# Weight loads moved from SyncE's queue to GpSimd's, and the order of the last four VectorE steps, in a fused attention and gated-FFN kernel

## The chip, the core and the metric

The kernel runs on one core of a Trainium2 chip. A core has TensorE (matrix products), VectorE, ScalarE and GpSimd (elementwise work and reductions) and SyncE, which here only issues DMAs. Each engine has a queue of its own, worked off in order; they meet at semaphores. SyncE, ScalarE and GpSimd can issue DMAs, and all DMAs of the core run on the same 16 DMA engines. The metric is the device time of one execution in microseconds (us).

## The reference

The output is `x + s * silu(r)`, with `x` of 2048 tokens by 640, `xn = layernorm(x)`, `s` an attention and `r` a small routed feed-forward block. All arrays are bf16.

```python
xn = _layernorm(x)
# A: attention against the last W = 512 rows of a cache, 32 heads of 192
q = (xn @ wq).reshape(B, Sq, 32, 192).transpose(0, 2, 1, 3)
scores = einsum("bhqd,bhkd->bhqk", q, k_cache[:, :, -512:]) * 192 ** -0.5
o = einsum("bhqk,bhkd->bhqd", softmax(scores), v_cache[:, :, -512:])
s = o.transpose(0, 2, 1, 3).reshape(B, Sq, 6144) @ wo
# B: the two tokens with the largest r go through a gated FFN of width 1536
r = xn @ w_r
idx = argsort(-r)[:, :2]
y = (silu(xn[idx] @ w_gate) * (xn[idx] @ w_up)) @ w_down
g = silu(xn + scatter_add(zeros, idx, y * sigmoid(r[idx])))
return x + s * g
```

## The kernel before

**The main loop.** The 32 heads are worked in 8 groups of 4. A group has 4 blocks of 512 tokens by 2 pairs of heads; each of these 64 steps is cut in two *halves* of 256 tokens, 128 halves in all, numbered k. A group is 16 halves. In half k TensorE makes the scores (`quad`, L296 to L303), VectorE the row maxima (L314), ScalarE the exponentials (L321, tile `pexp`). SyncE then issues one DMA transpose of `pexp` into `pT` (L327). Two halves later TensorE multiplies `pT` with the values (`o_products`, L339), VectorE scales the result (L353, `o_sb`), and SyncE issues its transpose `oT` (L357). Six halves later the output projection runs (`w_item`, L386 and L388) and VectorE adds it to `s_acc` (L394). The queries of the next step (L263, L268) are made in between. `pexp` has two buffers, so the exponentials of half k + 2 wait until the transpose of half k has landed.

**The order of the work** is written out by hand: `FIRST` and `LAST` list the steps of the ends as tokens, and in the loop between, each half runs what was put into the lists `mid[k]` and `bg[k]`. An engine's queue follows the order of the program. Nothing reorders it.

**SyncE's queue** carries nearly all DMAs: the transposes `pT`, `oT` and `kT` (the last turns the raw keys of the next group, L125), and the next group's loads, spread over the halves of the group: `wq_g` (L110), `k_raw` (L104), `v_sb` (L115), `wo_g` (L120). `kT`, `v_sb` and most of `wo_g` share the same few halves of each group.

**The routed block** is spread over halves 11 to 103. Its buffers are in two pools of one buffer each per tag; in the pool `moe_w` the candidates, the weights of each FFN block (`wgu`), those of the down projection (`wd`) and the broadcast result (`y_bc`) all have the tag `w`, that is, one buffer used in turn. GpSimd issues the gather of the two tokens (`xg`, L616, in half 33). Then, for each of three blocks `fb` of 512 columns, ten loads of 128 KB (`m_ffn_piece`, L626) fill `wgu`, one or two in a half, from halves 37, 44 and 52; the products with `wgu` (`m_ffn`, L666) run in halves 43, 51 and 58. Twelve loads of 160 KB (`m_wd_piece`, L684) fill `wd` in halves 59 to 66, and `m_down` uses it in half 68. `m_sum` then sends the result to all partitions by two DMAs of GpSimd (`y_d` L713, `y_bc` L715). From half 71 GpSimd adds it to `xn` (L719 to L723), from half 109 it multiplies and adds for the output (L782, L783).

**The end.** The last tokens' output rows are made by `last`: a `W` token is the projection (TensorE, L856), `m` the product with the gate `xn` (VectorE, L862, which reads the projection's PSUM), `a` the sum with `s_acc` on VectorE and `g` the same sum on GpSimd (both L866), each followed by SyncE's store (L867). The last 128 tokens are cut into two column halves, `127.0` and `127.1`, of 320 each.

The lists that place the loads:

```python
    pieces = {0: (2, 2, 2, 2, 2), 1: (1, 1, 2, 2, 2, 2), 2: (2, 2, 2, 2, 2)}
    for fb, (k0, km) in enumerate(((37, 43), (44, 51), (52, 58))):
        q = 0
        for h, n in enumerate(pieces[fb]):
            for _ in range(n):
                bg[k0 + h].append(m_ffn_piece(fb, q))
                q += 1
        mul, turn = m_ffn(fb)
        bg[km].append(mul)
        bg[km + 1].append(turn)
    q = 0
    for h, n in enumerate((1, 1, 1, 2, 2, 2, 2, 1)):
        for _ in range(n):
            bg[59 + h].append(m_wd_piece(q))
            q += 1
```

Of the kernel before, what the change touches and what calls it, by code (L numbers as in the profile page):

```python
# [21 lines left out]
def kernel(ctx, tc, A_x, A_k_cache, A_v_cache, A_wq, A_wo, B_x, B_w_r, B_w_gate, B_w_up, B_w_down, out):  # L22
    nc = tc.nc
    P = 128
# [4 lines left out]
    W = min(4096, max(256, Sk // 4))  # L29
# [113 lines left out]
    for _ in range(22):  # L143
# [5 lines left out]
        out=ident_f, in_=ident_f, compare_op=ALU.not_equal, fill=1.0, base=0,  # L149
# [373 lines left out]
    M = {}  # L523
# [96 lines left out]
    def m_ffn_piece(fb, q):  # L620
        def f():
            if q == 0:
                M["wgu"] = M["w"].tile([P, 2, DC, 512], BF16, name="wgu", tag="w")
            w, dc = divmod(q, DC)
            src = (B_w_gate, B_w_up)[w].rearrange("(c p) f -> p c f", p=P)
            nc.sync.dma_start(out=M["wgu"][:, w, dc, :], in_=src[:, dc, fb * 512:(fb + 1) * 512])  # L626
        return f

    def m_gather():
# [50 lines left out]
    def m_wd_piece(q):  # L680
        def f():
            if q == 0:
                M["wd"] = M["w"].tile([P, FC, D], BF16, name="wd", tag="w")
            nc.sync.dma_start(out=M["wd"][:, q, :], in_=B_w_down.rearrange("(c p) d -> p c d", p=P)[:, q, :])  # L684
        return f

    def m_sig():
# [58 lines left out]
    for fb, (k0, km) in enumerate(((37, 43), (44, 51), (52, 58))):  # L746
        q = 0
# [7 lines left out]
    q = 0  # L755
# [114 lines left out]
    S M.0 M.1 E.0 M.2 O.125.0 o.125.0 M.3 E.1 W.121.w m.121 a.121 R.127 O.125.1 o.125.1 C  # L870
    O.126.0 W.122.t O.126.1 o.126.0 m.122 o.126.1 g.122 W.123.w T.126 m.123
    O.127.0 o.127.0 O.127.1 o.127.1 g.123 W.124.t m.124 T.127 g.124 W.125.w m.125 g.125
    W.126.t m.126 g.126 W.127.0.h W.127.1.h m.127.0 a.127.0 m.127.1 a.127.1
    """.split()
    for token in LAST:
        last(token)
# [31 lines left out]
```

## Time and profile before

| | |
|---|---|
| median of 3 runs | 820.8 us (818.43 to 821.37) |
| the profiled execution | 818.35 us, its span 816.6 us |
| TensorE | 800.6 us busy, 98% |
| VectorE, ScalarE | 629.2 us (77%), 485.5 us (59%) |
| GpSimd | 203.1 us (25%) |
| DMA queue q1 (SyncE's) | 138.26 MB, 90.1% of the 16 engines' span |
| DMA queue q0 (GpSimd's) | 2.01 MB, 1.0% |
| SyncE's issues of wgu, wd | 30 of 128 KB, 12 of 160 KB; median 0.43 us each, landing 2.9 to 3.1 us after |
| SyncE's issue of pT | 126, 1.3 to 4.0 us, median 2.7; landing 4.2 to 7.6 us after, median 4.8 |

How to read the lines of the profile: times are us from the start of the span unless marked ns. PE is TensorE, PEld its weight loads, DVE VectorE, ACT ScalarE, POOL GpSimd, SP SyncE; a q behind a name is the engine's sequencer, which waits and issues. `L327` is a line of the kernel. `pT<-pexp` is what an instruction writes and reads. In a timeline a line has the start, the duration, the engine, line, operation, tiles and count, and in brackets the idle time of the engine before it and what ended that. In a line of stretches come the stretch, its length, then for PE, PEld, DVE, ACT and POOL the busy time and in brackets the number of instructions, then TensorE's granted clock, the DMA engines' busy share and GB/s. In the slices each digit is a fortieth of the span, in tenths (9 is 90% or more). A DMA queue has its packets, MB and share of the 16 engines' span.

### The profile page before, as it was taken

To read this page: it belongs to the slowest core of one execution; us is meant where nothing else is said; L and a number is where in the kernel's file an instruction comes from. 1 tells how busy PE (TensorE), PEld (TensorE's weight loads), DVE (VectorE), ACT (ScalarE), POOL (GpSimd) and SP (SyncE) were. 2 spreads that over 40 slices of the span, in tenths; PEclk is the share of its full clock that TensorE was granted. 3 is DMA by queue.
4 is the path that set the end of the run, shared out by engine and by line. 5 is a ranking of instruction groups with operands and counts; after the bars stand their busy time and mean duration, and the time that the engine had idled before them with its cause. 6 is when DMAs were issued, how large, how long until landed. Compare 5 with 4: busy or idle time off the path is not lost. (4 is left out here: it accounts for less than half of the span.)

```text
span 816.6 us, 15427 instructions
## 1 busy us (share of the span) xinstructions
PE 800.6 (98%) x5786; PEld 446.3 (55%) x5786; DVE 629.2 (77%) x1250; ACT 485.5 (59%) x1271; POOL 203.1 (25%) x151
## 2 busy tenths in 40 slices
PE   8889999999999999999999999999999999999997
PEld 4455555555555555555555555555555555555555
DVE  7988688887877776777676777777988877767886
ACT  5677565565565555556655665665676765655652
POOL 0001000000000000000000799999900001452533
PEclk9999999999999999999999999999999999999999
DMA  8889999989989999999999889887998879977984
GB/s 239 163 160 182 185 174 187 179 162 180 170 155 169 186 194 186 181 192 193 203 183 183 167 170 192 157 146 140 190 180 149 159 144 194 200 155 156 178 161 115
DMA packets 440427, 142.07 MB, mean 174 GB/s; under 512 B 413452, under 2 KB 439952, under 8 KB 440352
## 3 DMA queue, kind: packets, MB, share of 16 engines
q1 hardware_dynamic: 438720, 138.26, 90.1%
q0 software_dynamic: 688, 2.01, 1.0%
q8 instruction: 45, 0.74, 0.4%
q10 hardware_dynamic: 944, 0.82, 0.3%
q14 instruction: 30, 0.25, 0.1%
HBM read 39.98 MB, written 2.62 MB: 52 GB/s over the span
## 5 line engine op out<-in xcount | busy, mean ns | idle before, releaser
L321 ACT ACTIVATE pexp<-s,nm 128x512 bf16<-128x512 f32 x512 | 348.3, 691 | 257.3 <-DVE nm L314 162.2
L314 DVE TENSOR_REDUCE nm<-s 128x1 f32<-128x512 f32 x512 | 319.0, 683 | 56.0 <-PE s L303 55.9
L263 PE MATMUL q_ps<-xnT,wq_g 128*128 128x512 bf16 x945 | 234.7, 380 | 0.9 <-DMA xnT<-xn 0.7
L339 PE MATMUL o_ps<-v_sb,pT 128*128 128x192 bf16 x2048 | 210.3, 246 | 2.9 <-DMA pT<-pexp 1.3
L339 PEld LDWEIGHTS <-pT 128*128 128x128 bf16 x2048 | 173.1, 98 | 50.1 <-issue 6.1
L386 PE MATMUL w_ps<-wo_g,oT 128*128 128x512 bf16 x726 | 176.4, 379 | 0.0
L353 DVE TENSOR_TENSOR o_sb<-o_ps,lsum 128x384 bf16<-128x384 f32 x248 | 135.2, 545 | 47.0 <-PE o_ps L339 46.9
L263 PEld LDWEIGHTS <-wq_g 128*128 128x128 bf16 x945 | 80.3, 98 | 119.9 <-issue 50.1
L268 ACT ACTIVATE qT<-q_ps 128x512 bf16<-128x512 f32 x185 | 110.0, 596 | 40.1 <-PE q_ps L263 39.9
L394 DVE TENSOR_TENSOR s_acc<-s_acc,w_ps 128x640 f32<-128x640 f32 x96 | 78.8, 821 | 59.1 <-PE w_ps L388 58.8
L321 ACT ACTIVATION_READ_ACCUMULATOR pexp<-s,nm 128x1 f32 x512 | 106.2, 207 | 0.0
L386 PEld LDWEIGHTS <-oT 128*128 128x128 bf16 x726 | 69.1, 98 | 57.1
L297 PE MATMUL s<-kT,qT 128*128 128x512 bf16 x256 | 97.0, 379 | 1.9 <-ACT pexp L321 1.2
L296 PE MATMUL s<-kT,qT 128*128 128x512 bf16 x256 | 97.1, 379 | 0.6 <-ACT pexp L321 0.6
L302 PE MATMUL s<-kT,qT 64*128 64x512 bf16 x256 | 77.1, 381 | 0.0
L303 PE MATMUL s<-kT,qT 64*128 64x512 bf16 x256 | 77.1, 381 | 0.0
L388 PEld LDWEIGHTS <-oT 128*128 128x128 bf16 x726 | 50.7, 98 | 28.6
L722 POOL TENSOR_SCALAR yh<-y_bc,oh 128x640 bf16<-128x640 bf16 x32 | 61.3, 1916 | 3.3 <-DMA y_bc<-y_d 1.7
L388 PE MATMUL w_ps<-wo_g,oT 128*128 128x128 bf16 x726 | 60.3, 219 | 0.0
L713 POOL DMA_DIRECT2D y_d<-y_sb x1 | 0.6, 581 | 226.7 <-DVE y_sb L711 226.7
L723 POOL TENSOR_TENSOR xn<-xn,yh 128x640 bf16<-128x640 bf16 x32 | 44.6, 1394 | 2.7
L302 PEld LDWEIGHTS <-qT 64*128 64x128 bf16 x256 | 14.1, 94 | 56.3 <-issue 56.3
(134 smaller groups left out, 388.6 us busy)
## 6 DMA issues: line engine op xcount, KB each, us to landing
wo_g<-in_A_wo_dram SPq DMA_DIRECT2D x48, 160.0 KB, 2.9
wq_g<-in_A_wq_dram SPq DMA_DIRECT2D x35, 192.0 KB, 3.0
k_raw<-in_A_k_cache_dram SPq DMA_DIRECT2D x32, 192.0 KB, 3.0
v_sb<-in_A_v_cache_dram SPq DMA_DIRECT2D x32, 192.0 KB, 2.9
x_fin<-in_A_x_dram SPq DMA_DIRECT2D x16, 160.0 KB, 3.0
pT<-pexp SPq DMA_TRANSPOSE x130, 4.8
oT<-o_sb SPq DMA_TRANSPOSE x126, 3.2
wgu<-in_B_w_gate_dram SPq DMA_DIRECT2D x15, 128.0 KB, 3.0
```

The source lines that it names most:

```text
L263: nc.tensor.matmul(q_ps, lhsT=grp[g]["wq"][:, dc, col0:col0 + P], rhs=xnT[:, t5 * 4:(t5 + 1) * 4, dc, :], start=(dc == 0), stop=(dc == DC ...
L268: nc.scalar.activation(out=qT_of[i][:, c, :], in_=q_ps, func=ACT.Copy, scale=scale)
L296: nc.tensor.matmul(s0, lhsT=qT[:, 0, ssl], rhs=kp[:, :, 0, :], start=True, stop=False)
L297: nc.tensor.matmul(s1, lhsT=qT[:, 2, ssl], rhs=kp[:, :, 2, :], start=True, stop=False)
L302: nc.tensor.matmul(s0, lhsT=qT[0:64, 1, ssl], rhs=kp[0:64, :, 1, :], start=False, stop=True)
L314: nc.vector.tensor_reduce(out=nm_of[k][:, c:c + 1], in_=tiles[c // 2][c % 2], axis=AX.X, op=ALU.max, negate=True)
L321: nc.scalar.activation(out=pexp[:, u, hh, :], in_=tiles[u][hh], func=ACT.Exp, bias=nm[:, c:c + 1], scale=1.0, accum_out=l_of[k][:, c:c + 1])
L339: nc.tensor.matmul(o_ps[:, hh, :], lhsT=pT_of[k][:, u, hh, j, :], rhs=grp[g]["v"][:, 2 * pr + hh, j, :], start=(j == 0), stop=(j == NJ - 1))
L353: nc.vector.tensor_tensor(out=o_sb[:, u], in0=o_ps, in1=l_of[k][:, 2 * u:2 * u + 2].unsqueeze(2).to_broadcast([P, 2, Dh]), op=ALU.mult)
L386: nc.tensor.matmul(w_ps[:, 0:DA], lhsT=oT[:, c // 3, u % 2, c % 3, :], rhs=wo_g[:, c, 0:DA], start=(c == 0), stop=(c == CPG - 1))
L388: nc.tensor.matmul(w_ps[:, DA:D], lhsT=oT[:, c // 3, u % 2, c % 3, :], rhs=wo_g[:, c, DA:D], start=(c == 0), stop=(c == CPG - 1))
L394: nc.vector.tensor_tensor(out=s_acc[:, n, :], in0=s_acc[:, n, :], in1=w_ps, op=ALU.add)
```

## The change

The ten loads of each `wgu` set and the twelve of `wd` are issued by GpSimd instead of SyncE; their place in the program is the same. In `LAST` the product of the second column half comes before the sum of the first.

```diff
@@ m_ffn_piece
-            nc.sync.dma_start(out=M["wgu"][:, w, dc, :], in_=src[:, dc, fb * 512:(fb + 1) * 512])
+            nc.gpsimd.dma_start(out=M["wgu"][:, w, dc, :], in_=src[:, dc, fb * 512:(fb + 1) * 512])
@@ m_wd_piece
-            nc.sync.dma_start(out=M["wd"][:, q, :], in_=B_w_down.rearrange("(c p) d -> p c d", p=P)[:, q, :])
+            nc.gpsimd.dma_start(out=M["wd"][:, q, :], in_=B_w_down.rearrange("(c p) d -> p c d", p=P)[:, q, :])
@@ LAST
-    W.126.t m.126 g.126 W.127.0.h W.127.1.h m.127.0 a.127.0 m.127.1 a.127.1
+    W.126.t m.126 g.126 W.127.0.h W.127.1.h m.127.0 m.127.1 a.127.0 a.127.1
```

## The prediction

> **What bounds the kernel now.** I read four views, in this order: the page's slices, the busy time by stretch, the waits of the stretch in which the moved loads run, and the order of time around the one stall found there. First the slices, as tenths of the span: TensorE busy, its granted clock, then the DMA engines, and below them what the queues moved.
>
> ```profile
> PE   8889999999999999999999999999999999999997
> PEclk9999999999999999999999999999999999999999
> DMA  8889999989989999999999889887998879977984
> q1 hardware_dynamic: 438720, 138.26, 90.1%
> q0 software_dynamic: 688, 2.01, 1.0%
> ```
>
> TensorE is the bound, at full clock, with 16 us idle in all. Right behind it stand the 16 DMA engines: SyncE's queue q1 alone fills 90.1% of them. By stretch (us, TensorE busy first, the DMA share last but one):
>
> ```profile
> 249.00:283.00 34.00, 33.98 (x266) 19.23 (x263) 24.95 (x54) 19.88 (x54) 0.00 (x0) 1.00 0.99 180
> 298.00:330.00 32.00, 30.75 (x220) 16.91 (x218) 21.69 (x40) 17.82 (x49) 0.00 (x0) 1.00 1.00 185
> 385.00:440.00 55.00, 54.94 (x412) 30.95 (x410) 39.81 (x75) 32.55 (x87) 0.00 (x0) 1.00 1.01 194
> 500.00:550.00 50.00, 50.00 (x361) 28.03 (x359) 35.52 (x66) 29.98 (x81) 48.41 (x31) 1.00 0.89 158
> ```
>
> The first three hold the moved loads, the last holds none: with them the DMA engines are full (0.99 to 1.01), without them they have a tenth to spare (0.89). TensorE loses time in one of them only, 1.25 us. These are the lines around that loss: ScalarE's last read of the softmax of one half (an iteration of the main loop, some 6 us), SyncE's queue, then who waits for the transpose pT.
>
> ```profile
> 300.39 0.22 ACT L321 ACTIVATION_READ_ACCUMULATOR pexp<-s,nm 128x1 f32 x1
> ...
> 302.25 1.23 SPq L357 DMA_TRANSPOSE oT<-o_sb  x1
> 303.54 0.57 SPq L115 DMA_DIRECT2D v_sb<-in_A_v_cache_dram  x1
> 304.16 0.42 SPq L120 DMA_DIRECT2D wo_g<-in_A_wo_dram  x1
> 304.63 0.43 SPq L626 DMA_DIRECT2D wgu<-in_B_w_gate_dram  x1
> 305.17 2.99 SPq L327 DMA_TRANSPOSE pT<-pexp  x1
> ...
> 311.33 0.83 PE L339 MATMUL o_ps<-v_sb,pT 128*128 128x192 bf16 x8 [1.25 <-DMA pT<-pexp]
> 311.39 0.69 ACT L321 ACTIVATE pexp<-s,nm 128x512 bf16<-128x512 f32 x1 [3.98 <-DMA pT<-pexp]
> ```
>
> The input was ready at 300.61, but SyncE, back to back, issued at 305.17: 4.56 us late. It landed 6.1 us later, at 311.29. **The cushion.** An undisturbed pT is issued 0.02 us after its input and lands in 4.8 us (its median), here 305.43. It came 5.86 us late and TensorE lost 1.25, so a pT may be 4.6 us late for nothing; beyond that each microsecond is TensorE's. Two groups later, in the same place with no moved load:
>
> ```profile
> 495.64 0.22 ACT L321 ACTIVATION_READ_ACCUMULATOR pexp<-s,nm 128x1 f32 x1
> ...
> 497.76 2.27 SPq L327 DMA_TRANSPOSE pT<-pexp  x1
> ```
>
> Input at 495.86, issue at 497.76, landing 5.5 us on, at 503.26: 2.6 us later than undisturbed (500.68). So the loads and the k transpose of that place use 2.6 us of the cushion by themselves. SyncE's issue of a pT took 1.3 to 4.0 us, median 2.7; the 2.99 above is the queue being held by full DMA engines.
>
> **The change, part by part.** *Removed from SyncE:* 42 issues of 0.43 us (their median), 18 us spread over 249 to 435, each ahead of a pT. Nearly all of it lies beside TensorE's work. On the path is the 1.25 us loss, which I count as gained. The bytes stay: the DMA engines still carry 30 x 128 KB and 12 x 160 KB.
>
> *Added to GpSimd:* 42 issues at 0.57 us (the median of its nine stores), 24 us. GpSimd is empty there: before its y_d it idles 226.7 us, from the gather's issue at 220.46. The wd issues, about 7 us from 378, are over before y_d at 448, so nobody queues behind them.
>
> *Moved in time.* This is the costly part. In SyncE's queue the 42 loads are dosed, one or two in a half, because each stands between transposes in program order. GpSimd has nothing between them, so only the buffer holds them. All of wgu, wd, the candidates and y_bc share the one moe_w buffer, so a set starts when its last reader ends: set 0 behind the gather at 221.5, set 1 when the first gate product ends (282.11 + 0.73 = 282.8), set 2 at 333.15 + 0.73 = 333.9, wd at 377.33 + 0.73 = 378.1. Each set then goes out in 10 or 12 issues, 6 to 7 us.
>
> *Price of a burst*, in time of all 16 DMA engines. From above: q0 took 1.0% of 816.6 = 8.2 us for 2.01 MB, so 0.53 us for 128 KB and 0.67 us for 160 KB: 5.3 us a wgu set, 8.0 us wd. From below: the excess of the DMA share over 0.89 in the stretches above, 0.10 x 34 = 3.4 us for wgu and 0.12 x 55 = 6.6 us for wd. Neither end excludes the other; I take the middle, 4.4 and 7.3. A backlog then stands ahead of the transposes, and shrinks by the tenth to spare, 0.6 us a half.
> - Set 0 and set 2 fall where no k transpose or v load runs: 4.4 against 4.6, no loss (0 to 0.7 each).
> - Set 1 falls on the place that uses 2.6 itself: 4.4 + 2.6 - 4.6 = 2.4 us (1.4 to 3.3).
> - wd is the same place a group on; it starts two halves ahead of the peak, which absorbs about 1 us: 7.3 + 2.6 - 1.0 - 4.6 = 4.3 us (3.6 to 5.0).
>
> Sum 6.7 (5.0 to 9.7). Below nothing: were transposes never held by q0, all four are 0.
>
> A packet row decides that. Beside GpSimd's stores at 759.32 and 771.46, pT issued at 758.00 and 770.13 landed in 5.3 and 5.6 us; beside those at 765.92 and 783.61 in 4.3 and 4.3. So 160 KB on the other queue cost a transpose up to 1.0 to 1.3 us, not less than its 0.67. I take the burst as served first.
> On arbitration the Trainium skill (DMA: Bandwidth & Descriptors, section Queues, rings and completion order) says that each DMA engine takes turns between queues a whole packet at a time. The page's q0 row, 2.01 MB in 688 packets, shows large ones; q1 has 138.26 MB in 438720. By that rule the large packets get most of each turn, which speaks against the change and gives the same sum.
>
> **The tail.** Now VectorE does product 0 (811.13), sum 0 (811.66, 1.41 us, beside GpSimd's sum, which ends at 812.72), product 1 (812.99), sum 1 (813.50 to 813.99). After: product 1 as soon as its matmuls end at 811.80, about 812.0 to 812.5; sum 0 held until about 813.1 as now; sum 1 0.49 us, to 813.6. Gain 0.4 us. Ends: 0.5 (a whole product of 0.48 off the path), or a loss of 0.5 if the product too is held by GpSimd.
>
> *Sum:* +6.7 - 1.25 - 0.4 = **+5.0 us**. The profiled execution took 818.35 (span 816.6 and 1.75 around it), which gives 823.4. It was 2.45 below the median of 820.8, so against the median 825.8. For this case alone: 5.0 - 1.25 - 0.5 = +3.3 to 9.7 - 1.25 + 0.5 = +9.0, so 824.1 to 829.8.
>
> **Rivals.**
> *Hidden (no change):* the bursts do not delay transposes, because the loads get only what q1 leaves. For it: the stores at 765.92 and 783.61 cost nothing, and every product has its weights 40 us early, so late loads harm nobody. Against: the DMA share of 1.0. Time 820.8 - 1.25 - 0.4 = 819.2.
> *Trickle (no change):* GpSimd cannot write its requests fast enough, so a set leaks out over many halves. Decided where an issue lasts over 3 us: 10 x 3 = 30 us is the dosing of now. Against it: issues of 0.54 to 1.03 us under the same VectorE load. Time again 819.2.
> The Trainium skill (SBUF — State Buffer, section SBUF: two separate sides) says that VectorE's two-port operations lock GpSimd out of writing descriptors. No wait here shows it.
> *Issue-bound (faster):* SyncE's instructions, not the DMA engines, make the transposes late. Place: 283 to 312, where its queue never rests. If the 42 issues are the cause, pT's lateness falls by 0.9 to 1.2 us a half, the 1.25 us and ScalarE's 3.98 us wait go; if that wait had been on the path, 820.8 - 3.98 - 0.4 = 816.4. It decides if, with wgu gone, pT's issue drops to 1.3 to 1.8 us. Against: issues of 2.99 beside a share of 1.00.
> *Heavier turns (slower):* a load on q0 costs a transpose 1.0 us per 160 KB, as in the two slow landings, 0.8 per 128 KB: sets 8, 8, 8 and 12. Losses 3.4 + 6.0 + 3.4 + 9.0 = 21.8, less 1.65: 841. Half of that mark-up gives some 833.
>
> **How the numbers follow.** Forecast 0.50, hidden 0.20, trickle 0.07, issue-bound 0.07, heavier turns 0.16. A difference below 0.5% (4.1 us) can hardly be told from none. Slower by over that (above 824.9): four fifths of the forecast case, 0.40, and the heavier case 0.16: 0.56. Same: the rest of the forecast, 0.10, hidden and trickle, 0.27, and a little of issue-bound, 0.02: 0.39. Faster 0.05. The range runs from the hidden case less half a microsecond of spread, 818.7, to half the mark-up, 833; it leaves out issue-bound and the upper half of heavier turns, 0.15.
>
> **What would show it.** Right: wgu on q0, all ten issues of a set inside some 6 us at 221, 283 and 334, wd at 378; DMA share near 0.9 in 249 to 283; TensorE waits for pT around 295 to 312 and 390 to 410, 2 to 5 us each. Hidden: no such wait and pT landings below 7 us. Trickle: issues far apart. Issue-bound: pT issued at once everywhere. Tail: product 1 before sum 0, the end 0.4 us earlier behind the last matmul. I am wrong if the DMA engines carry more with two queues than with one, so that 1.00 was no ceiling.

## The result and the profile after

The changed kernel takes 828.59 us (median of 6 runs, 825.55 to 832.21) against 819.29 us for the kernel before beside it. The ratio is 1.012, with a 95% interval of 1.0093 to 1.0146: it is slower. The profiled execution took 827.15 us with a span of 825.4 us, 8.8 us more than before.

The page's slices and DMA queues of the kernel after:

```profile
PE   8889999999999999999899999999999999999996
PEclk9999999999999999999999999999999999999999
DMA  8889999899998999999997889887998879988884
q1 hardware_dynamic: 432672, 132.36, 86.1%
q0 software_dynamic: 2704, 7.91, 4.2%
```

The moved 5.9 MB are now on GpSimd's queue q0. TensorE has one visible dent, in the slice around 400 us. By stretch (length, then the busy time of PE, PEld, DVE, ACT, POOL, then clock, DMA share, GB/s), first a stretch of the kernel before, then four of the kernel after:

```profile
200.00:249.00 49.00, 49.00 (x351) 27.38 (x350) 38.62 (x92) 28.98 (x79) 1.62 (x2) 1.00 0.88 158
```

```profile
200.00:249.00 49.00, 47.79 (x339) 26.47 (x341) 37.63 (x90) 27.77 (x75) 7.02 (x12) 1.00 0.99 180
249.00:283.00 34.00, 33.82 (x250) 19.42 (x250) 25.06 (x53) 20.77 (x57) 0.00 (x0) 1.00 0.87 159
298.00:330.00 32.00, 29.50 (x211) 16.51 (x212) 21.25 (x39) 18.14 (x48) 0.00 (x0) 1.00 0.96 182
385.00:440.00 55.00, 51.22 (x366) 28.18 (x369) 37.23 (x70) 29.42 (x81) 2.14 (x4) 1.00 1.00 193
```

In 249 to 283, where SyncE had issued the first set, the DMA share fell from 0.99 to 0.87. The set had moved into 200 to 249, where the share rose from 0.88 to 0.99. TensorE loses time in the first, third and fourth stretch of the kernel after. These lines of GpSimd's timeline show the whole of the first burst and the start of the other three; the rest of those is left out at the dots:

```profile
220.32 1.03 POOL L616 DMA_INDIRECT xg<-in_A_x_dram,idx_i  x1 [19.09 <-DVE idx_i L614]
221.37 2.74 POOL L626 DMA_DIRECT2D wgu<-in_B_w_gate_dram  x5
224.06 1.65 POOL L626 DMA_DIRECT2D wgu<-in_B_w_up_dram  x3
227.49 1.07 POOL L626 DMA_DIRECT2D wgu<-in_B_w_up_dram  x2 [1.79 <-DMA wgu<-in_B_w_gate_dram]
284.19 2.65 POOL L626 DMA_DIRECT2D wgu<-in_B_w_gate_dram  x5 [55.62 <-PE gu_ps L666]
...
336.54 2.64 POOL L626 DMA_DIRECT2D wgu<-in_B_w_gate_dram  x5 [46.15 <-PE gu_ps L666]
...
380.71 4.22 POOL L684 DMA_DIRECT2D wd<-in_B_w_down_dram  x8 [37.59 <-PE gu_ps L666]
...
```

The four bursts start at 221.4, 284.2, 336.5 and 380.7, each released by the gather or by the last gate product that read the buffer. A set of wgu goes out in 6.2 to 7.2 us, wd in 9.1 (380.71 to 389.81). And these are TensorE's waits that follow, from its timeline:

```profile
236.63 0.83 PE L339 MATMUL o_ps<-v_sb,pT 128*128 128x192 bf16 x8 [1.00 <-DMA pT<-pexp]
300.55 0.83 PE L339 MATMUL o_ps<-v_sb,pT 128*128 128x192 bf16 x8 [1.59 <-DMA pT<-pexp]
313.68 0.83 PE L339 MATMUL o_ps<-v_sb,pT 128*128 128x192 bf16 x8 [0.81 <-DMA pT<-pexp]
397.77 0.83 PE L339 MATMUL o_ps<-v_sb,pT 128*128 128x192 bf16 x8 [2.47 <-DMA pT<-pexp]
403.96 0.83 PE L339 MATMUL o_ps<-v_sb,pT 128*128 128x192 bf16 x8 [0.47 <-DMA pT<-pexp]
411.33 0.83 PE L339 MATMUL o_ps<-v_sb,pT 128*128 128x192 bf16 x8 [0.58 <-DMA pT<-pexp]
```

None follows the third burst. The wait at 311.33 of the kernel before is now the one at 313.68. SyncE's queue shows how a burst gets at a transpose (the issue at 289.27 is of the pT that TensorE waits for at 300.55):

```profile
289.27 7.57 SPq L327 DMA_TRANSPOSE pT<-pexp  x1
296.94 1.80 SPq L357 DMA_TRANSPOSE oT<-o_sb  x1
```

It was issued on time, 0.02 us after its input, but the issue itself took 7.57 us (4.0 was the longest before). The burst ran beside it, and the DMA share from 284 to 297 was 1.16, against 1.06 before. The pT for the wait at 397.77 was held up twice, first by the issue of the kT transpose ahead of it, then by its own; its input was ready at 385.78:

```profile
383.77 5.33 SPq L125 DMA_TRANSPOSE kT<-k_raw  x1
389.22 6.56 SPq L327 DMA_TRANSPOSE pT<-pexp  x1
```

The end, on VectorE:

```profile
818.25 0.49 DVE L862 TENSOR_TENSOR fin_t<-w_e,xn 128x320 f32<-128x320 f32 x1
818.96 0.49 DVE L862 TENSOR_TENSOR fin_t<-w_e,xn 128x320 f32<-128x320 f32 x1 [0.21 <-PE w_e L856]
819.37 1.23 DVE L866 TENSOR_TENSOR fin_o<-fin_t,s_acc 128x320 bf16<-128x320 f32 x2
```

From the first of the two products to the last sum's end it is 2.35 us (818.25 to 820.60) instead of 2.86 (811.13 to 813.99). But the span ends 4.8 us behind that sum instead of 2.6. What fills this is GpSimd's drain, the instruction behind its last sum. Three drains close GpSimd's program; durations are min/median/max in ns, and the longest is the one in question. Before:

```profile
L903 POOLq DRAIN  x3: 46/97/2890, 811.1 to 816.3; - x3
```

and after:

```profile
L903 POOLq DRAIN  x3: 46/97/6325, 818.3 to 825.1; - x3
```

So the 8.8 us of the profiled execution are three terms. TensorE's last matmul ends 7.1 us later (818.92 against 811.80), VectorE gives back 0.5, and the end behind the last sum is 2.2 longer.

### The profile page after: what moved, and what is told of

Same layout as the page of the kernel before. It is cut to its first block, busy times and chain, and to the rows that moved or that the text cites. A ratio compares the mean times of both kernels' runs of the same rounds, so it can differ in the third digit from the quotient of the medians.

```text
span 825.4 us, 15374 instructions
## 1 busy us (share of the span) xinstructions
PE 798.1 (97%) x5718; PEld 445.6 (54%) x5786; DVE 629.9 (76%) x1250; ACT 484.9 (59%) x1271; POOL 225.5 (27%) x193
## 5 line engine op out<-in xcount | busy, mean ns | idle before, releaser
L386 PE MATMUL w_ps<-wo_g,oT 128*128 128x512 bf16 x661 | 163.4, 379 | 3.4
L783 POOL TENSOR_TENSOR s_acc<-s_acc,x_fin 128x640 f32<-128x640 f32 x16 | 22.4, 1398 | 63.0 <-DMA x_fin<-in_A_x_dram 62.5
```

The costliest lines, as they stand in the source:

```text
L386: nc.tensor.matmul(w_ps[:, 0:DA], lhsT=oT[:, c // 3, u % 2, c % 3, :], rhs=wo_g[:, c, 0:DA], start=(c == 0), stop=(c == CPG - 1))
```

## The experiments

The theory is that of the prediction: ten or twelve loads at once hold the transposes up, and TensorE pays for what exceeds a cushion of 4.6 us. The rivals after the result: loads on another queue hold transposes up by their turns, at any pace; and the loss goes with the number of loads moved. The drain was new and needed a cause of its own. Four kernels (`tail_only`, `move_only`, `paced`, `tiny42`) ran on one chip beside 25 runs of the kernel before, the other four on another beside 23. In `move_only`, `wd_only` and `sp_burst` the profiled execution is the fastest of four, so their traces show somewhat less than the medians.

**One part alone: the end.** The loads stay on SyncE's queue, the tokens of the end are in the new order.

> Edit: only the order of the last VectorE steps is changed, the loads stay on SyncE's queue. Both theories: within 0.1% of before. In the profile the second product comes ahead of the first sum, and the last sum ends 3.5 us after the last projection's first matmul instead of 4.0 (810.01 to 813.99 before, 817.13 to 820.60 after). No change in TensorE's waits for pT in the middle, and GpSimd's last drain ends 1.3 us after its last sum, as before.

Measured: 817.36 us against 817.69, ratio 0.9993 (0.9984 to 1.0003): no difference that can be told. The last sum ends 812.72, 3.46 us behind the first matmul of the last projection (809.26), as expected. The waits differed more than expected: the one at 311.33 was 0.6 instead of 1.25 us, without an edit near it, so this wait varies by half a microsecond between executions.

**One part alone: the loads.** The changed kernel with the old order of the end.

> Edit: only the 42 loads are moved to GpSimd's queue, the end is in the old order. Both theories: the whole loss of the change and half a microsecond more, 1.1 to 1.3% slower than before. TensorE waits for pT at about 237, 300, 314 and four times at 398 to 417 us; GpSimd's last drain ends 4 to 5 us after its last sum.

Measured: 830.69 us, ratio 1.0166 (1.0147 to 1.0186), more than the 1.1 to 1.3% expected. Of the seven expected waits the trace has three: 0.90 us at 300.66, 0.64 at 313.64 and 4.84 at 400.11. Near 237 TensorE also loses about 0.7 us, there with only a weight load put down as waiting for pT. The four waits expected behind wd are one longer wait, and a stretch of lower granted clock goes with it. That is taken up with `wd_only`, where it is clean.

**The burst or the queue.** Every half's loads wait for a small GpSimd copy that reads that half's row maxima.

```diff
+    def m_pace(k):
+        def f():
+            pace = M["s"].tile([P, 4], FP32, name="pace")
+            nc.gpsimd.tensor_copy(out=pace, in_=nm_of[k])
+        return f
...
         for h, n in enumerate(pieces[fb]):
+            bg[k0 + h].append(m_pace(k0 + h))
             for _ in range(n):
...
     for h, n in enumerate((1, 1, 1, 2, 2, 2, 2, 1)):
+        bg[59 + h].append(m_pace(59 + h))
         for _ in range(n):
```

> Edit: the changed kernel, with a copy of 4 columns on GpSimd ahead of each half's loads, which reads that half's row maxima; so the 42 loads are on GpSimd's queue but go out one or two a half, as SyncE had them. Burst theory (the loss comes from ten or twelve loads at once): TensorE's waits for pT fall from 7 us in sum to under 2, and what is left is GpSimd's longer drain at the end, about 2 us: 0.0 to 0.4% slower than before. Rival (a load on GpSimd's queue holds up transposes whenever it goes out, by taking turns with them): the waits stay, spread out, and the loss stays over 0.7%.

Measured: 819.06 us, ratio 1.0018 (1.0008 to 1.0028). GpSimd's timeline and the stretches of this kernel:

```profile
300.41 0.19 POOL L623 COPY pace<-nm 128x4 f32<-128x4 f32 x1 [4.09 <-DVE nm L314]
300.88 1.06 POOL L632 DMA_DIRECT2D wgu<-in_B_w_gate_dram  x2 [0.28 <-issue]
307.02 0.19 POOL L623 COPY pace<-nm 128x4 f32<-128x4 f32 x1 [5.08 <-DVE nm L314]
307.49 0.54 POOL L632 DMA_DIRECT2D wgu<-in_B_w_gate_dram  x1 [0.28 <-issue]
```

```profile
298.00:330.00 32.00, 31.89 (x225) 17.74 (x226) 22.85 (x43) 18.59 (x49) 5.00 (x12) 1.00 1.07 199
385.00:440.00 55.00, 54.73 (x407) 30.96 (x411) 39.84 (x75) 32.51 (x87) 7.17 (x18) 1.00 1.05 206
```

The same 42 loads on the same queue, dosed: TensorE waits for no pT at all between 200 and 470, not even the 1.25 us of the kernel before. Transposes land a little later in the two stretches shown, 5.2 and 5.3 us after their issue in the median against 4.9 before, which stays within the cushion. The rival of turns at any pace is out as the cause of the loss. What is left of the loss is the drain, 6.3 us here too.

**A burst on SyncE's own queue.** The loads stay with SyncE, each set in one half; set 0 also starts three halves earlier than before.

```diff
-    pieces = {0: (2, 2, 2, 2, 2), 1: (1, 1, 2, 2, 2, 2), 2: (2, 2, 2, 2, 2)}
-    for fb, (k0, km) in enumerate(((37, 43), (44, 51), (52, 58))):
+    pieces = {0: (10,), 1: (10,), 2: (10,)}
+    for fb, (k0, km) in enumerate(((34, 43), (44, 51), (52, 58))):
...
-    for h, n in enumerate((1, 1, 1, 2, 2, 2, 2, 1)):
+    for h, n in enumerate((12,)):
```

> Edit: the kernel before, all loads on SyncE's queue, but each set goes out at once, the ten of wgu in halves 34, 44 and 52, the twelve of wd in half 59. Burst theory (loads at once are enough, whatever the queue): TensorE waits 4 to 9 us for pT in sum, behind sets 1 and wd above all, 0.4 to 1.0% slower than before; GpSimd's last drain stays at 2.9 us. Rival (the turns between two queues make the loss): within 0.2% of before.

Measured: 823.5 us, ratio 1.0072 (1.0055 to 1.0089); the drain is 2.888 us. Waits on pT between 200 and 470, as engine, line, what it waited for, then us in sum, times, longest:

```profile
ACT pexp L321 <- DMA pT<-pexp: 16.4, 5, 5.2
PEld L339 <- DMA pT<-pexp: 7.1, 5, 2.8
PE o_ps L339 <- DMA pT<-pexp: 3.5, 3, 2.3
```

The burst alone, without a second queue and without GpSimd, costs 0.7%. The expected 4 to 9 us of TensorE's waits were at their lower end or below (3.5 for the matmuls, 7.1 for the weight loads ahead of them). But this burst reaches the transposes in another way than that of the change. SyncE's queue before the longest of these waits:

```profile
390.68 6.72 SPq L684 DMA_DIRECT2D wd<-in_B_w_down_dram  x12
397.50 3.05 SPq L327 DMA_TRANSPOSE pT<-pexp  x1
```

Here the transpose stands behind the 6.7 us that SyncE needs to issue the twelve loads, and its own issue is of ordinary length. So this run shows that a burst ahead of a pT costs time on one queue too; it does not show that DMA engines filled by it are the reason. For the change that rests on the issues of 7.57 and 6.56 us beside its bursts, against at most 4.1 us anywhere with the same loads paced.

**Half a burst.** The loads of w_gate and every second one of wd are on GpSimd's queue.

```diff
-            nc.gpsimd.dma_start(out=M["wgu"][:, w, dc, :], in_=src[:, dc, fb * 512:(fb + 1) * 512])
+            (nc.gpsimd if w == 0 else nc.sync).dma_start(out=M["wgu"][:, w, dc, :], in_=src[:, dc, fb * 512:(fb + 1) * 512])
...
-            nc.gpsimd.dma_start(out=M["wd"][:, q, :], in_=B_w_down.rearrange("(c p) d -> p c d", p=P)[:, q, :])
+            (nc.gpsimd if q % 2 == 0 else nc.sync).dma_start(out=M["wd"][:, q, :], in_=B_w_down.rearrange("(c p) d -> p c d", p=P)[:, q, :])
```

> Edit: the changed kernel, but of each wgu set only the five loads of w_gate, and of wd only every second load, are on GpSimd's queue; the others go out dosed on SyncE's. Theory of a cushion of 4.6 us: half a burst (2.2 and 3.7 us) fits under it or nearly, so the waits for pT are under 2 us in sum; GpSimd's drain of 21 more DMAs, at 82 ns each, takes 4.6 us and is hidden but for 0.2 us: between 0.15% faster and 0.2% slower. Rival (the loss goes with the number of loads moved): half of the change's, 0.5 to 0.8% slower.

Measured: 817.54 us, ratio 0.9992 (0.9983 to 1.0001). In the whole stretch one wait of TensorE's matmuls for pT is left:

```profile
404.16 0.83 PE L339 MATMUL o_ps<-v_sb,pT 128*128 128x192 bf16 x8 [0.69 <-DMA pT<-pexp]
```

Half of the loads moved, none of the loss: the cost is not proportional to the loads. It sets in somewhere between half a burst and a whole one. The drain:

```profile
L903 POOLq DRAIN  x3: 46/97/4605, 810.9 to 816.1; - x3
```

4.6 us, as expected from 82 ns for each DMA.

**The drain alone.** The kernel before, with 42 tiny DMAs on GpSimd's queue, unpaced, which move 2 KB each.

```diff
+    def m_tiny(q):
+        def f():
+            if q == 0:
+                M["tiny"] = M["s"].tile([P, 42, 8], BF16, name="tiny")
+            nc.gpsimd.dma_start(out=M["tiny"][:, q, :], in_=B_w_gate[0:P, q * 8:(q + 1) * 8])
+        return f
...
+    for q in range(42):
+        bg[37 + q * 30 // 42].append(m_tiny(q))
```

> Edit: the kernel before, with 42 more DMAs on GpSimd's queue in halves 37 to 66, each of 128 rows of 16 bytes, to a tile that nothing reads. It asks what lengthens GpSimd's last drain (1.3 us behind its last sum before, 4.7 us after the change). If it is the number of DMAs that GpSimd issued: 4 to 5 us here too, the span ends some 2 us later behind the last store, and 0.2 to 0.3% slower than before, without waits for pT in the middle beyond the 1.25 us. If it is their bytes, or the waits that the changed kernel had: 1.3 us as before, and no slower.

Measured: 819.51 us against 817.69, ratio 1.0021 (1.0012 to 1.0031), with one wait for pT of 0.6 us in the middle.

```profile
L912 POOLq DRAIN  x3: 46/97/6320, 811.1 to 818.0; - x3
```

6.32 us, as after the change, with hardly a byte moved. The drain goes with the number of DMAs that GpSimd has issued, not with what they carry.

**Only wd.** The changed kernel with wgu back on SyncE's queue.

> Edit: the changed kernel with wgu back on SyncE's queue; only the twelve loads of wd are on GpSimd's. Theory: the wd burst alone costs TensorE 4 to 5 us between 385 and 420, 0.4 to 0.6% slower than before; GpSimd's drain with 28 DMAs takes 2.89 + 12 x 0.082 = 3.9 us, which does not reach the end. Rival for the drain (it has two values, not a price for each DMA): 2.9 or 6.3 us.

Measured: 825.87 us against 817.73, ratio 1.0105 (1.0086 to 1.0123), more than the 0.4 to 0.6% expected. The drain is where the price for each DMA puts it (there are 15 such DMAs in the kernel before and 27 here; the expectation counted one too many, but not the twelve added):

```profile
L903 POOLq DRAIN  x3: 46/97/3870, 817.3 to 822.4; - x3
```

The rest is in TensorE's timeline and in the stretches around it (the granted clock last but two):

```profile
396.85 0.83 PE L339 MATMUL o_ps<-v_sb,pT 128*128 128x192 bf16 x8 [4.12 <-DMA pT<-pexp]
```

```profile
392.00:396.80 4.80, 0.73 (x4) 0.12 (x2) 1.84 (x4) 0.00 (x0) 0.00 (x0) 1.00 1.21 182
396.80:397.80 1.00, 0.90 (x9) 0.83 (x11) 0.08 (x1) 0.89 (x3) 0.00 (x0) 1.00 0.66 114
397.80:401.20 3.40, 3.40 (x16) 2.01 (x16) 0.99 (x2) 2.38 (x7) 0.00 (x0) 0.50 1.02 137
401.20:405.00 3.80, 3.80 (x28) 2.01 (x27) 3.09 (x7) 1.36 (x5) 0.00 (x0) 1.00 0.98 207
```

A wait of 4.12 us, near the 4.3 forecast for wd. Then, a microsecond later, TensorE is granted half its clock for 3.4 us, which costs another 3.4 x 0.5 = 1.7 us. Both together, 5.8 us, are nearly the whole of the 6.0 us that TensorE loses there against the kernel before. The Trainium skill (TensorE: Matmul & The Clock Gate, section Part 1: The HAM clock gate) says that the clock falls to one half after an idle window of about 3.4 us and comes back after as long a busy one. This trace agrees, with a wait of 4.12 us and 3.4 us at 0.50; the 2.47 us wait of the changed kernel's profile was followed by no such stretch. No run here shows how long a wait must be for it.

**A second queue without bursts and without GpSimd.** The loads stay in their old halves, issued by ScalarE, with the new order of the end.

```diff
-            nc.sync.dma_start(out=M["wgu"][:, w, dc, :], in_=src[:, dc, fb * 512:(fb + 1) * 512])
+            nc.scalar.dma_start(out=M["wgu"][:, w, dc, :], in_=src[:, dc, fb * 512:(fb + 1) * 512])
...
-            nc.sync.dma_start(out=M["wd"][:, q, :], in_=B_w_down.rearrange("(c p) d -> p c d", p=P)[:, q, :])
+            nc.scalar.dma_start(out=M["wd"][:, q, :], in_=B_w_down.rearrange("(c p) d -> p c d", p=P)[:, q, :])
```

> Edit: the kernel before with the new order of the end, the 42 loads in their old halves, but issued by ScalarE. If two queues carry more than one, as the paced loads on GpSimd's queue suggest, TensorE waits for no pT, and GpSimd's drain stays at 2.9 us: 0.1 to 0.3% faster than before. Rival: ScalarE's issues, some 0.5 us each between the exponentials, delay the softmax and the gain is lost: 0.0 to 0.3% slower.

Measured: 816.53 us against 817.73, ratio 0.9984 (0.9976 to 0.9993), faster than both kernels. TensorE waits for no pT between 200 and 470, the drain is 2.890 us.

```profile
298.00:330.00 32.00, 31.84 (x229) 18.10 (x231) 22.92 (x42) 19.23 (x53) 0.00 (x0) 1.00 0.99 194
385.00:440.00 55.00, 54.73 (x408) 30.84 (x411) 38.69 (x73) 32.40 (x88) 0.00 (x0) 1.00 1.10 203
```

The 42 issues on ScalarE cost TensorE nothing that can be seen. The profiled span is 814.8 us, 1.8 less than that of the kernel before, which fits the 1.25 us wait and the 0.5 us of the end; by the medians it is 1.2 us. There was hardly more to be had in this stretch, where TensorE was nearly always busy already.

## Why the prediction was right, and what it missed

The direction and the mechanism were right: slower, by bursts. The size was short: +5.0 us forecast (+3.3 to +9.0 for that case alone), +8.8 measured in the profiled execution and +9.3 by the medians. Of the 8.8, the 2.2 us behind the last sum have a cause that the prediction does not name. Its mechanism accounts for at most 7.1 - 0.5 = 6.6 us.

- *The start of the bursts* was forecast from the buffer and the queue as 221.5, 282.8, 333.9 and 378.1; they came at 221.4, 284.2, 336.5 and 380.7, the later ones shifted by what TensorE had already lost.
- *The cushion of 4.6 us* held. The pT for 300.55 would have landed, undisturbed, 4.82 us behind its input at 289.25, so at 294.07. It was used at 300.55, 6.5 us later, and TensorE waited 1.59: 4.9 were free. For 397.77 the input was at 385.78, lateness 7.2, wait 2.47: 4.7 free.
- *Sets 1 and 2 and wd* were sized well for the profiled execution. Set 1: 2.4 forecast, 1.59 + 0.81 = 2.4 measured. Set 2: 0, and none. wd: 4.3 forecast; from the start of that place to half 62 the shift grows from 2.4 to 6.6 us (410.49 became 417.09), 4.2. That it comes so close is in part luck: the same twelve loads brought one wait of 4.84 us in `move_only` and of 4.12 in `wd_only`, each with a stretch at half the clock, which the prediction does not have.
- *Set 0* was undersized: no loss forecast (0 to 0.7), a wait of 1.0 us measured. Its pT was 5.7 us late (input at 226.15, undisturbed landing 230.97, use at 236.63), so the burst cost a little more than the 5.3 us of the upper bound, not the middle of 4.4 that was taken. The queue's row says the same of all four: q0's share grew from 1.0 to 4.2% of the span, some 26 us, where the upper bounds add up to 24.
- *The 1.25 us wait* was counted as gained. The paced and the ScalarE version have none, so it goes with the loads out of SyncE's queue. In the changed kernel 0.81 us are waited at the same place, which the sum above puts down to set 1; no run tells whether a part of it is the old wait. `tail_only` and `tiny42`, with the loads where they were, have only 0.6 us there.
- *The end* gained 0.5 in the profile, forecast 0.4; in the medians of `tail_only` it can't be told from nothing.
- *The step that failed* is the 42 issues added to GpSimd, which the sum has at nothing because nobody queues behind them. The program's own end does. 42 more DMAs lengthen GpSimd's drain from 2.89 to 6.32 us, 82 ns each; it begins when GpSimd's last sum is issued, so before it was over at 814.04, 1.8 us before the last store let SyncE through (815.8), and now it ends last, 1.9 us behind SyncE. With the 0.3 us that SyncE's own end took longer this is the 2.2 us at the end.
- Some 0.5 us of TensorE's shift came after 570 us, at places where the kernel before is short of the cushion too (the loads of `x_fin` near 706). No run separates it from the half microsecond by which such waits vary.

Of the rivals, *issue-bound* was right in one thing: relieving SyncE does take the wait at 311 away. It does not bring more than that. *Heavier turns* is out, since TensorE waits for none of the transposes beside the paced loads, and half a burst costs nothing. *Hidden* fell with the 7 us of waits, *trickle* with issues of 0.54 us. The doubt in the prediction's last sentence, that two queues might carry more than one, is not settled: in 298 to 330 and 385 to 440 the share was 1.00 and 1.01 with one queue, 1.07 and 1.05 paced on GpSimd's, 0.99 and 1.10 on ScalarE's, and in both of these TensorE awaited no transpose, but the kernel before reached 1.06 in 360 to 385 as well. The burst of the change came to 1.16 in 284 to 297, so 1.00 is not the most that this share can show.

Open is how the change's other executions divide. The profiled one had a mean granted clock of 0.999 and no slow stretch in the middle; the other five had 0.993 to 0.996 and took 825.55 to 832.21 us. A wait of 4.12 us in `wd_only` and one of 4.84 in `move_only` went with a stretch at half the clock, so longer waits in these executions are a likely reason, but they have no trace here and it is not shown.

## What to carry to other kernels

Loads in a busy queue are dosed by what stands between them; on an idle engine's queue only the buffer holds them, so they go out together. Look up what else needs the DMA engines in that moment, and how late it may be. If a second queue is wanted, keep the dose, and count what the issuing engine still does at the very end of the program.

## What the runs showed of the hardware that was not expected

- GpSimd's last drain grows by 82 ns for each DMA that it issued anywhere in the program: 2.89, 3.87, 4.61 and 6.32 us for 15, 27, 36 and 57 in all, whether they carried 160 KB or 2 KB.
- GpSimd sent eight loads of a set without a wait and held the ninth (set 1: the tenth) until an earlier one had landed, 1.79 us at 227.49. This need not be a limit of the engine: in the trace its DMAs use eight semaphores in turn, and each waits for the DMA that had the same one. Twelve loads on SyncE's queue went out without such a gap (`sp_burst`).
- A transpose's issue on SyncE lasted up to 7.57 us beside a burst on another queue, and 9.58 in `wd_only`; 4.0 was the longest in the kernel before.
- A TensorE wait of 4.12 us was followed by 3.4 us at half the granted clock: by the working above it cost about 40% more than its length.
